# Router logits as float32r products of high and low halves, with the maximum in the adding instruction

## The chip, the core and the metric

The kernel runs on one core of a Trainium2 chip. The time is that of the device, in microseconds (us), from the start of the program to its end; lower is better. Engines: PE (TensorE, matrix products; PEld is its weight load), DVE (VectorE), ACT (ScalarE), POOL (GpSimd) and SP (the queue that issues most DMAs).

## The reference

Three layers one after the other, all in float32: attention with a sliding window and sinks, a mixture of experts with one expert for each token, and a feed-forward layer.

```python
# attention: batch 2, 8 heads, sequence 768, head size 64; keep = 4 sink keys or 128 nearest keys
scores = np.where(keep, scale * np.matmul(q, k.transpose(0, 1, 3, 2)), -1e9)
a = softmax(scores); x = np.matmul(a, v)            # then reshaped to 1536 tokens x 512
# mixture of experts: 8 experts, 512 -> 1024 -> 512
xn = x / (norm(x) + 1e-6); en = expert_emb / (norm(expert_emb) + 1e-6)
logits = xn @ en.T / tau
expert_idx = np.argmax(logits, axis=1)
gate_w = softmax(logits)[chosen]
out[mask] = gate_w[mask, None] * (np.maximum(x[mask] @ w1[e], 0.0) @ w2[e])
# feed-forward: 512 -> 2048 -> 512
h = out @ w_in; y = np.maximum(0.01 * h, h) @ w_out
```

The change is in the router: `logits` for 1536 tokens and 8 experts, and their maximum.

## The kernel before

The program is one stream of instructions per engine. Attention takes the first 140 us or so. It works through 96 items (batch, group of four heads, block of 128 queries, head), and `value` joins four of them to a block. A block of 128 tokens is complete when its second group of heads is done; that makes 12 token tiles, t = 0 to 11. While PE works on scores (L276), transposes of the probabilities (L299) and products with the values (L317, L320) of later items, the router of a finished tile is worked in: three steps later `router_turn`, five steps later `router_logits`.

- `router_turn` (L722) transposes the tile's 512 columns in four pieces into one PSUM tile `xTp` of the pool `ps_t` (4 buffers, shared with all other transposes). ACT copies it to `xT` in SBUF as float32 (L732), then squares the tile for its norm (L739).
- `router_logits` (L742) multiplies the four pieces of `xT`, as stationary operand, with the embeddings `embT` (8 columns) into a PSUM tile `lg` of the pool `ps_sc` (3 buffers, shared with the scores). The profile records each float32 product as two weight loads and two matmuls, so a tile has eight of each. One DVE instruction (L751) copies the logits to SBUF and takes the maximum `top`; L753 to L755 make the index and the one-hot row `oh`, L757 adds it to the count `cum`.
- The last tile (t = 11) is in `HALF`: its first two pieces are transposed and copied eight steps or more earlier, as soon as its first group of heads is done (L337, L338). Only the other half is left for the end.
- After tile 7, `choose` picks the expert that has most tokens so far and has its weights loaded. After tile 9 and after tile 11, `router_rank` (L760, products `rk`) numbers the tokens within their experts. At the end `rank_experts` (L862) counts tokens of each expert from `cum` and `oh` of the last tile (products `cnt`, L874 and L875) and sorts the experts; its result `eid` lets SP load the weights of the next experts.
- The first expert's products (`first_unit`, `ahead`; L1330 writes `hp`) are placed behind the last logits. Some products with no use (`fill`, L841) stand in the gaps.

The order on each engine is fixed before the run. In attention a scheduler settles it from dependencies and its own estimates; an engine then executes strictly in this order. After attention the order on PE is that of the code. The products of attention's scores and most of the experts' and the feed-forward layer's are float32r already, as three products of high and low halves (L1230); ACT writes the high half rounded and DVE the difference.

Of the kernel before, what the change touches and what calls it, by code (L numbers as in the profile page):

```python
# [7 lines left out]
F32 = mybir.dt.float32  # L8
F32R = mybir.dt.float32r
# [6 lines left out]
ALU = mybir.AluOpType  # L16
# [5 lines left out]
P = 128  # L22
# [3 lines left out]
E = 8  # L26
# [4 lines left out]
NTT = NT // P  # L31
# [19 lines left out]
EASE = (4, 5, 6)  # L51
AHEAD = 1
BETWEEN = ("down", 1, 2)
HALF = [NTT - 1]
MAN = set()
STIR = {s: 2 for s in range(9)}
UNITS = [(0, 0, 0, 6), (0, 1, 0, 6), (1, 0, 0, 2), (1, 1, 0, 2), (1, 0, 2, 6), (1, 1, 2, 6)]
# [91 lines left out]
def attention(c, ctx):  # L149
# [109 lines left out]
    def later(n, fn):  # L259

        if n == 0:
            return fn()
        after.append((step[0] + n, c.uid(), fn))
# [47 lines left out]
    def value(b, g, i):  # L311
# [23 lines left out]
        later(1, finish)  # L335
        half = t in HALF
        if g == 0 and half:  # L337
            later(3, lambda: router_turn(c, t, None, (0, 1)))  # L338
        if g == 1:
            if t >= NTT - 2:  # L340
                later(3, lambda: fill(c, c.pst, "t", 1))
            later(3, lambda: router_turn(c, t, None, (2, 3) if half else (0, 1, 2, 3)))
            later(5, lambda: router_logits(c, t))
            if t == T0 - 1:
                later(5, lambda: choose(c))
            if t in RANKS:
                t0 = RANKS[RANKS.index(t) - 1] + 1 if RANKS.index(t) else 0
                if t == NTT - 1:
                    later(7, lambda: rank_experts(c))
                later(7, lambda: router_rank(c, t0, t + 1))  # L350
                if t == T0 - 1:
                    later(7, lambda: choose_rows(c))
            if t == NTT - 1:
                later(3, lambda: first_unit(c))
                later(5, lambda: ahead(c))
# [15 lines left out]
    turn = {(0, 0): group_turns(0, 0)}  # L371
    router_tables(c)
    setting = router_setup(c)
    stir(7)
    n = len(items)
# [242 lines left out]
def router_setup(c):  # L618

    nc, tc = c.nc, c.tc  # L620
    cp = c.const
    rp, emb, tau = c.embs
    sq = rp.tile([E, DM], BF16, name="sq")
    ss = rp.tile([E, 1], F32, name="ss")
    nc.scalar.activation(out=sq, in_=emb, func=AF.Square, accum_out=ss)
    yield
    nrm = norm(c, rp, ss, [E, 1], "e")
    yield
    nc.vector.tensor_scalar(out=nrm, in0=nrm, scalar1=1e-6, scalar2=tau, op0=ALU.add, op1=ALU.mult)
    nc.vector.reciprocal(out=nrm, in_=nrm)  # L630
    nc.vector.tensor_scalar(out=emb, in0=emb, scalar1=nrm, scalar2=None, op0=ALU.mult)
    yield
    t = c.pst.tile([P, 4, E], F32, tag="t", name="embT_ps")
    for kk in range(4):
        nc.tensor.transpose(t[:, kk, :], emb[:, kk * P:(kk + 1) * P], c.ident[0:E, 0:E])
    c.embT = cp.tile([P, 4, E], F32, name="embT")
    nc.vector.tensor_copy(c.embT, t)


def router_tables(c):  # L640
# [65 lines left out]
def norm(c, pool, ss, shape, nm):  # L706

    V = c.nc.vector
    y = pool.tile(shape, F32, name=f"ny_{nm}")
    q = pool.tile(shape, F32, name=f"nq_{nm}")  # L710
    yi = y.bitcast(I32)
    V.tensor_scalar(out=yi, in0=ss.bitcast(I32), scalar1=1, scalar2=None, op0=ALU.logical_shift_right)
    V.tensor_scalar(out=yi, in0=yi, scalar1=float(0x1fbd1df5), scalar2=None, op0=ALU.add)
    for _ in range(3):
        V.reciprocal(out=q, in_=y)
        V.tensor_tensor(out=q, in0=q, in1=ss, op=ALU.mult)
        V.tensor_tensor(out=y, in0=q, in1=y, op=ALU.add)
        V.tensor_scalar(out=y, in0=y, scalar1=0.5, scalar2=None, op0=ALU.mult)
    return y


def router_turn(c, t, pool=None, parts=(0, 1, 2, 3)):  # L722

    nc = c.nc
    pool = pool or c.pst
    x = c.x[t].rearrange("p h d -> p (h d)")
    tp = pool.tile([P, len(parts), P], F32, tag="t", name=f"xTp{c.uid()}")
    for k, kk in enumerate(parts):
        turned = nc.tensor.transpose(tp[:, k, :], x[:, kk * P:(kk + 1) * P], c.ident)  # L729
    if parts[0] == 0:  # L730
        c.xT[t] = c.rt.tile([P, 4, P], F32, tag="xT" if parts[-1] == 3 else "xTh", name=f"xT{c.uid()}", bufs=2 if parts[-1] == 3 else 1)
    first = nc.scalar.copy(out=c.xT[t][:, parts[0]:parts[-1] + 1], in_=tp)  # L732
    if parts[-1] == 3:
        c.x.pop(t)
        c.xT[t] = c.xT[t], turned
        c.turned = turned
        sq = c.rt.tile([P, DM], BF16, tag="sq", name=f"sq{c.uid()}", bufs=1)
        with c.tc.issue_after(first.ins):
            nc.scalar.activation(out=sq, in_=x, func=AF.Square, accum_out=c.ss[:, t:t + 1])  # L739


def router_logits(c, t, pool=None):  # L742

    nc = c.nc
    xT, turned = c.xT.pop(t)
    lp = (pool or c.psc).tile([P, E], F32, tag="sc", name=f"lg{c.uid()}")
    with c.tc.issue_after(turned.ins):
        for kk in range(4):
            c.logged = nc.tensor.matmul(lp, lhsT=xT[:, kk, :], rhs=c.embT[:, kk, :], start=(kk == 0), stop=(kk == 3))  # L749
    lg, top, idx, oh = c.lg[:, t, :], c.top[:, t], c.idx[:, t:t + 1], c.oh[:, t, :]  # L750
    nc.vector.tensor_scalar(out=lg, in0=lp, scalar1=0.0, scalar2=None, op0=ALU.add, op1=ALU.max, accum_out=top)  # L751
    hit = c.rt.tile([P, E], F32, tag="hit", name=f"hit{c.uid()}")
    nc.vector.scalar_tensor_tensor(out=hit, in0=lg, scalar=top, in1=c.em8, op0=ALU.is_equal, op1=ALU.mult)  # L753
    nc.vector.tensor_reduce(out=idx, in_=hit, axis=AX.X, op=ALU.min)
    nc.vector.tensor_scalar(out=oh, in0=c.em8, scalar1=idx, scalar2=None, op0=ALU.is_equal)  # L755
    if t + 1 < NTT:
        nc.vector.tensor_tensor(out=c.cum[:, t + 1, :], in0=c.cum[:, t, :], in1=oh, op=ALU.add)  # L757
# [941 lines left out]
```

## Time and profile before

| | |
|---|---|
| median of 3 runs | 594.13 us (592.95 to 597.09) |
| profiled execution, whole time | 593.38 us |
| its span | 591.6 us |
| PE busy | 579.3 us, 98% of the span |
| PEld busy | 516.1 us, 87% |
| DVE busy | 375.1 us, 63% |
| ACT busy | 278.1 us, 47% |
| POOL busy | 64.7 us, 11% |
| chain that ended last | PE 86%, DVE 4%, issue 3%, DMA 3%, ACT 2% |

The span is the part of the profiled execution that the trace covers; 1.8 us of its time lie outside. Busy shares are means over stages with different limits, so the stretch in question has to be looked at by itself. A busy PE is not a PE at its peak: matmuls are pipelined, and their ends are modelled. The chain shows when each instruction's turn came, so a run of n instructions over a time gives the pace of one.

### The profile page before, as it was taken

How to read it: one execution, taken by the hardware profiler on the slowest of the kernel's cores; microseconds unless marked ns; L12 is line 12 of the kernel's file. 1: busy time of each engine (PE TensorE's matmuls, PEld its weight loads, DVE VectorE, ACT ScalarE, POOL GpSimd, SP SyncE). 2: the span in 40 equal slices, each digit the busy share in tenths (PEclk: the TensorE clock that was granted, in tenths of full speed). 3: DMA queues.
4: the chain of work that ended last, by engine and by line, in shares of the span. 5: the costliest groups of instructions: out<-in, count | busy, mean ns of one | idle time of the engine just before them, and what ended most of it. 6: DMA issues, size and time to landing. Idle time of an engine off the chain costs nothing.

```text
span 591.6 us, 9764 instructions
## 1 busy us (share of the span) xinstructions
PE 579.3 (98%) x3504; PEld 516.1 (87%) x3505; DVE 375.1 (63%) x903; ACT 278.1 (47%) x532; POOL 64.7 (11%) x195
## 2 busy tenths in 40 slices
PE   8999999999999999999999999999999999999995
PEld 5998999999999998899999888888888888888884
DVE  7999699776689966887991799954322223322240
ACT  4878687663476436744552545423322222322220
POOL 6223012121301000010000000000100001100001
PEclk9999999999999999999999999999999999999999
DMA  7646142082295569999977500000100000100001
GB/s 160 154 95 130 61 113 65 24 285 90 77 315 168 157 173 302 350 376 364 377 268 226 202 1 0 2 0 19 54 0 1 0 1 24 48 0 1 0 20 58
DMA packets 75178, 70.44 MB, mean 119 GB/s; under 512 B 41236, under 2 KB 57620, under 8 KB 75120
## 3 DMA queue, kind: packets, MB, share of 16 engines
q1 hardware_dynamic: 72736, 63.07, 34.4%
q0 software_dynamic: 2096, 6.64, 3.4%
q8 instruction: 30, 0.49, 0.3%
q14 instruction: 28, 0.23, 0.1%
q10 hardware_dynamic: 288, 0.00, 0.0%
HBM read 63.41 MB, written 6.29 MB: 118 GB/s over the span
## 4 chain that ended last, share of the span: by engine, by line
PE 86%; DVE 4%; issue 3%; DMA 3%; ACT 2%; SPq 1%; POOL 0%; DVEq 0%; POOLq 0%; ACTq 0%
PE hp L1230 29%; PE acc L1230 28%; PE xp L317 6%; PE hp L1330 4%; PE acc L1348 4%; PE sc L276 4%; PE tp L299 3%; PE lg L749 2%; DMA slot_first<-in_moe_w 1%; PE tq L206 1%; PE xp L320 1%; PE xTp L729 1%; PE tr L1218 1%; PE tk L206 1%; DVE head_k L217 1%
## 5 line engine op out<-in xcount | busy, mean ns | idle before, releaser
L1230 PE MATMUL acc<-slot,h 128*128 128x512 f32 x588 | 142.7, 390 | 0.0
L1230 PE MATMUL hp<-fxT,slot 128*128 128x512 f32 x576 | 137.1, 389 | 0.0
L1230 PEld LDWEIGHTS acc<-slot,h 128*128 128x128 f32 x588 | 109.6, 188 | 22.3
L1230 PEld LDWEIGHTS hp<-fxT,slot 128*128 128x128 f32 x576 | 108.1, 188 | 22.4
L1595 DVE TENSOR_TENSOR lk<-hp,lk 128x512 f32<-128x512 f32 x48 | 32.9, 689 | 97.5 <-ACT lk L1594 97.3
L1594 ACT ACTIVATE lk<-hp 128x512 f32<-128x512 f32 x48 | 28.5, 598 | 110.3 <-PE hp L1230 104.5
L285 ACT ACTIVATE p<-p,los 128x288 f32<-128x288 f32 (+2 forms) x96 | 46.1, 506 | 15.3 <-DVE los L281 14.3
L1150 DVE TENSOR_TENSOR slot<-slot_raw,slot 128x1024 fp32r<-128x1024 f32 x36 | 42.9, 1220 | 4.7 <-ACT slot L1149 4.6
L276 PE MATMUL sc<-head_k,head_q 128*128 128x288 f32 (+1 forms) x192 | 44.9, 332 | 0.6 <-DVE los L281 0.4
L1629 POOL DMA_INDIRECT out_y<-y,sid x12 | 11.7, 978 | 304.2 <-DVE y L1628 282.9
L317 PE MATMUL xp<-v,pt 128*128 128x65 f32 x352 | 44.2, 269 | 0.6 <-DVE x L331 0.5
L317 PEld LDWEIGHTS xp<-v,pt 128*128 128x128 f32 x352 | 42.8, 191 | 1.0 <-PE rk L766 0.6
L1597 DVE TENSOR_TENSOR h<-lk,h 128x512 fp32r<-128x512 f32 x43 | 29.5, 690 | 18.1 <-ACT h L1596 17.9
L1596 ACT CAST h<-lk 128x512 fp32r<-128x512 f32 x43 | 26.7, 622 | 29.2 <-DVE lk L1595 29.2
L1149 ACT CAST slot<-slot_raw 128x1024 fp32r<-128x1024 f32 x36 | 36.0, 1049 | 0.0
L1348 PE MATMUL acc<-h,slot_raw 128*128 128x184 f32 (+2 forms) x192 | 33.8, 320 | 0.1
L276 PEld LDWEIGHTS sc<-head_k,head_q 128*128 128x128 f32 x192 | 29.0, 190 | 3.7 <-DVE los L281 1.3
L1348 PEld LDWEIGHTS acc<-h,slot_raw 128*128 128x128 f32 x192 | 30.7, 190 | 0.4 <-DVE yT L1354 0.4
L1230 PE MATMUL acc<-h,slot 128*128 128x352 f32 (+1 forms) x192 | 30.7, 309 | 0.0
L299 PE MATMUL tp<-ident,p 128*128 128x128 f32 x176 | 29.8, 274 | 0.3 <-ACT pt L302 0.2
L1230 PEld LDWEIGHTS acc<-h,slot 128*128 128x128 f32 x192 | 28.7, 188 | 0.0
L1246 POOL DMA_INDIRECT rows<-xd,ids x15 | 15.5, 1030 | 112.0 <-PE tr L1218 103.3
(294 smaller groups left out, 910.3 us busy)
## 6 DMA issues: line engine op xcount, KB each, us to landing
slot_raw<-in_moe_w SPq DMA_DIRECT2D x48, 512.0 KB
slot_first<-in_moe_w SPq DMA_DIRECT2D x16, 512.0 KB
slot_wide<-in_moe_w_in SPq DMA_DIRECT2D x8, 1024.0 KB
slot_wide<-in_moe_w_out SPq DMA_DIRECT2D x8, 1024.0 KB
raw_k<-in_k SPq DMA_DIRECT2D x32, 96.0 KB
raw_q<-in_q SPq DMA_DIRECT2D x32, 96.0 KB
xd<-x SPq DMA_DIRECT2D x12, 256.0 KB
v<-in_v SPq DMA_DIRECT2D x12, 192.0 KB
```

The lines of the kernel that those rows point to most:

```text
L276: nc.tensor.matmul(sc[:, 0:w], lhsT=qt[:, half, i * P:(i + 1) * P], rhs=kt[:, off:off + w], start=half == 0, stop=half == 1)
L285: c.raised = nc.scalar.activation(out=p, in_=p, func=AF.Exp, scale=-1.0, bias=lo)
L299: nc.tensor.transpose(u.t[:, h % 2, n, :], u.p[:, h, o:o + P], c.ident)
L317: nc.tensor.matmul(xp[:, h, :], lhsT=u.pt[h // 2][:, h % 2, n, :], rhs=vT[b, g][:, kb, h, :], start=h == 0 and n == 0, stop=h == 3 and i < ...
L1149: nc.scalar.copy(out=sl.g[0], in_=raw)
L1150: nc.vector.tensor_tensor(out=sl.g[1], in0=raw, in1=sl.g[0].bitcast(F32), op=ALU.subtract)
L1230: c.nc.tensor.matmul(out, lhsT=a[x], rhs=b[y], start=first and n == 0, stop=last and n == 2)
L1348: nc.tensor.matmul(acc[k], lhsT=g[:, f % 2, k * P:(k + 1) * P], rhs=h, start=f == 0, stop=f == nf - 1)
L1594: nc.scalar.activation(out=raw, in_=hp, func=AF.Copy, scale=0.01)
L1595: nc.vector.tensor_tensor(out=raw, in0=hp, in1=raw, op=ALU.max)
L1596: x = nc.scalar.copy(out=h[:, 0, :], in_=raw)
L1597: y = nc.vector.tensor_tensor(out=h[:, 1, :], in0=raw, in1=h[:, 0, :].bitcast(F32), op=ALU.subtract)
```

## The change

The embeddings are kept twice more: `embR` holds their high half (rounded to float32r) and their low half (the rest) side by side, 16 columns for each of the four pieces. This is done once (two DVE instructions).

For each tile ACT writes the transposed tile's high half instead of a float32 copy, and a new DVE instruction (L737 of the changed kernel) subtracts it from `xTp` to make the low half. The logits come from eight float32r products: four with the high half of x against both halves of the embeddings (128x16), four with the low half of x against the high embeddings (128x8), added in the first 8 of the 16 columns. Then ACT copies the other 8 columns to `lg` (L759), and one DVE instruction with an accumulator (L760) adds both parts and takes the maximum, in place of L751.

`xT` is twice as large and has one buffer instead of two. `HALF` is empty: the last tile is transposed whole after its second group of heads.

```diff
-HALF = [NTT - 1]
+HALF = []
...
     c.embT = cp.tile([P, 4, E], F32, name="embT")
+    c.embR = cp.tile([P, 4, 2, E], F32R, name="embs")
     nc.vector.tensor_copy(c.embT, t)
+    nc.vector.tensor_copy(c.embR[:, :, 0], t)
+    nc.vector.tensor_tensor(out=c.embR[:, :, 1], in0=t, in1=c.embR[:, :, 0].bitcast(F32), op=ALU.subtract)
...
-        c.xT[t] = c.rt.tile([P, 4, P], F32, tag="xT" if parts[-1] == 3 else "xTh", name=f"xT{c.uid()}", bufs=2 if parts[-1] == 3 else 1)
-    first = nc.scalar.copy(out=c.xT[t][:, parts[0]:parts[-1] + 1], in_=tp)
+        c.xT[t] = c.rt.tile([P, 2, 4, P], F32R, tag="xT", name=f"xT{c.uid()}", bufs=1)
+    hi, lo = (c.xT[t][:, h, parts[0]:parts[-1] + 1] for h in range(2))
+    first = nc.scalar.copy(out=hi, in_=tp)
+    nc.vector.tensor_tensor(out=lo, in0=tp, in1=hi.bitcast(F32), op=ALU.subtract)
...
-    lp = (pool or c.psc).tile([P, E], F32, tag="sc", name=f"lg{c.uid()}")
+    lp = (pool or c.psc).tile([P, 2, E], F32, tag="sc", name=f"lg{c.uid()}")
     with c.tc.issue_after(turned.ins):
         for kk in range(4):
-            c.logged = nc.tensor.matmul(lp, lhsT=xT[:, kk, :], rhs=c.embT[:, kk, :], start=(kk == 0), stop=(kk == 3))
+            nc.tensor.matmul(lp.rearrange("p h e -> p (h e)"), lhsT=xT[:, 0, kk, :], rhs=c.embR[:, kk].rearrange("p h e -> p (h e)"),
+                             start=(kk == 0), stop=False)
+        for kk in range(4):
+            c.logged = nc.tensor.matmul(lp[:, 0], lhsT=xT[:, 1, kk, :], rhs=c.embR[:, kk, 0], start=False, stop=(kk == 3))
     lg, top, idx, oh = c.lg[:, t, :], c.top[:, t], c.idx[:, t:t + 1], c.oh[:, t, :]
-    nc.vector.tensor_scalar(out=lg, in0=lp, scalar1=0.0, scalar2=None, op0=ALU.add, op1=ALU.max, accum_out=top)
+    nc.scalar.copy(out=lg, in_=lp[:, 1])
+    nc.vector.tensor_tensor_reduce(out=lg, in0=lp[:, 0], in1=lg, scale=1.0, scalar=-3.0e38, op0=ALU.add, op1=ALU.max, accum_out=top)
```

The scheduler orders attention anew, so lines shift in the whole stage. Three places matter. The first is DVE in the middle of attention, around the end of one tile's index work and the start of the next block's scores (`p` is the masked score tile, `sc` the scores in PSUM). Before:

```order
L755 TENSOR_SCALAR oh<-em_263,idx 128x8
L217 TENSOR_TENSOR head_k_149<-tk_1444,head_k_149 64x384
L217 TENSOR_TENSOR head_k_151<-tk_1444,head_k_151 64x384
L757 TENSOR_TENSOR cum<-cum,oh 128x8
L281 ISA p_1472,los<-sc_1473,ma 128x288
```

And in the changed kernel, at the corresponding place:

```order
L764 TENSOR_SCALAR oh<-em_263,idx 128x8
L737 TENSOR_TENSOR xT_1482<-xTp_1477,xT_1482 128x512
L766 TENSOR_TENSOR cum<-cum,oh 128x8
L281 ISA p_1494,los<-sc_1495,ma 128x288
L281 ISA los 128x1
```

A subtraction of 128x512 now stands in DVE's queue ahead of the masked scores, whose buffers PE waits to get back.

The second place is DVE at the end of attention, around the values of the last tile (`xp_2453` before, `xp_2512` after; `x` is the finished tile, `rec` the reciprocal). Before:

```order
L753 SCALAR_TENSOR_TENSOR hit_2421<-lg,top,em_263 128x8
L754 TENSOR_REDUCE idx<-hit_2421 128x1
L755 TENSOR_SCALAR oh<-em_263,idx 128x8
L757 TENSOR_TENSOR cum<-cum,oh 128x8
L329 TENSOR_SCALAR rec_2458<-xp_2453 128x4
L769 TENSOR_TENSOR sel_2433<-rk_2430,oh 128x16
L330 RECIPROCAL rec_2458<-rec_2458 128x4
L770 TENSOR_REDUCE r<-sel_2433 128x2
L331 TENSOR_TENSOR x_2254<-xp_2453,rec_2458 128x256
```

After:

```order
L762 SCALAR_TENSOR_TENSOR hit_2479<-lg,top,em_263 128x8
L763 TENSOR_REDUCE idx<-hit_2479 128x1
L737 TENSOR_TENSOR xT_2507<-xTp_2502,xT_2507 128x512
L764 TENSOR_SCALAR oh<-em_263,idx 128x8
L329 TENSOR_SCALAR rec_2517<-xp_2512 128x4
L766 TENSOR_TENSOR cum<-cum,oh 128x8
L330 RECIPROCAL rec_2517<-rec_2517 128x4
L778 TENSOR_TENSOR sel_2491<-rk_2488,oh 128x16
L331 TENSOR_TENSOR x_2305<-xp_2512,rec_2517 128x256
```

The subtraction for tile 10 (`xT_2507`) stands ahead of the one-hot row of tile 9, and so ahead of everything that finishes tile 11.

The third place is PE over the same time, from the values of the last tile to its logits. Before:

```order
L729 MATMUL xTp_2444<-ident,x_2207 128x128 x2
L317 MATMUL xp_2453<-v_1608,pt_2384 128x65 x2
L317 MATMUL xp_2453<-v_1608,pt_2402 128x65 x2
L766 LDWEIGHTS tri
L766 MATMUL rk_2430<-oh,tri 128x16
L766 LDWEIGHTS ones
L766 MATMUL rk_2430<-cum,ones 128x16
L749 MATMUL lg_2459<-embT,xT_2449 128x8 x4
L729 MATMUL xTp_2476<-ident,x_2254 128x128 x2
L1218 MATMUL tr_2482<-ident,slot_rows_134 128x128 x4
L749 MATMUL lg_2488<-embT,xT_2284 128x8 x4
```

After:

```order
L317 MATMUL xp_2512<-v_1641,pt_2455 128x65 x2
L775 LDWEIGHTS tri
L775 MATMUL rk_2488<-oh,tri 128x16
L775 LDWEIGHTS ones
L775 MATMUL rk_2488<-cum,ones 128x16
L754 MATMUL lg_2518<-embs,xT_2507 128x16 x4
L757 MATMUL lg_2518<-embs,xT_2507 128x8 x4
L732 MATMUL xTp_2540<-ident,x_2305 128x128 x2
L1227 MATMUL tr_2550<-ident,slot_rows_134 128x128 x4
L754 MATMUL lg_2556<-embs,xT_2545 128x16 x4
L757 MATMUL lg_2556<-embs,xT_2545 128x8 x4
```

The sequence is the same with logits in two groups of four; the first two transposes of the last tile, which stood earlier in attention, now stand just ahead of the logits of tile 9 (`lg_2468`, not shown).

## Rows read from the trace of the kernel before

**Rows 1.** The page's first line: length of the span.

```profile
span 591.6 us, 9764 instructions
```

**Rows 2.** Stretches: length, busy PE, PEld, DVE, ACT, POOL, clock, DMA share, GB/s.

```profile
60.00:70.00 10.00, 10.00 (x87) 9.79 (x86) 5.87 (x24) 5.59 (x14) 1.24 (x6) 1.00 0.19 64
70.00:110.00 40.00, 40.00 (x347) 39.13 (x346) 36.22 (x153) 32.74 (x79) 9.06 (x26) 1.00 0.32 81
...
125.00:140.00 15.00, 15.00 (x128) 14.51 (x128) 8.78 (x42) 9.59 (x26) 0.59 (x2) 1.00 0.72 251
```

**Rows 3.** Chain that ended last, in order: start us, length us, engine and line.

```profile
60.10 0.44 PE xTp L729 x4
60.53 1.73 PE xp L317 x16
...
63.20 0.79 PE lg L749 x8
...
212.29 0.36 PE ipp L1019 x12
...
222.34 1.43 PE hp L1230 x12
```

**Rows 4.** Groups by shape to 240 us: busy us, mean ns | idle before.

```profile
L276 PEld LDWEIGHTS sc<-head_k,head_q 128*128 128x128 f32 x192 | 29.0, 190 | 3.7 <-DVE los L281 1.3 <-DVE head_q L229 0.7 <-issue 0.3
...
L749 PEld LDWEIGHTS lg<-embT,xT 128*128 128x128 f32 x96 | 11.7, 192 | 0.1
...
L1230 PE MATMUL hp<-slot,mxT 128*128 128x256 f32 x48 | 6.6, 287 | 0.0
...
L732 ACT COPY xT<-xTp 128x512 f32<-128x512 f32 x11 | 6.4, 585 | 4.6 <-PE xTp L729 4.5
...
L281 DVE CUSTOM_DVE_ANT_0 p<-sc,m 128x128 f32<-128x128 f32 x16 | 4.5, 283 | 2.2 <-PE sc L276 2.1
L309 ACT COPY ps<-sk 128x128 f32<-128x128 f32 x16 | 4.2, 264 | 3.3 <-PE sk L307 3.2
...
L362 PEld LDWEIGHTS <-warm 128*128 128x128 bf16 x29 | 2.9, 116 | 3.0 <-issue 1.4 <-DVE warm L248 1.2
...
L1223 DVE TENSOR_TENSOR slot_big<-tr,slot_big 128x512 fp32r<-128x512 f32 x3 | 2.0, 679 | 0.0
```

**Rows 5.** The same chain at the end of attention, from tile 9's logits.

```profile
139.10 0.79 PE lg L749 x8
139.90 0.35 PE xTp L729 x2
140.25 0.84 PE xp L317 x8
...
142.02 0.43 PE xTp L729 x2
142.45 0.44 PE tr L1218 x4
142.89 0.79 PE lg L749 x8
...
144.14 1.03 PE hp L1330 x8
145.17 0.01 PE cnt L875
```

**Rows 6.** DVE in order of time there: start us, length us, line, operation.

```profile
141.54 0.42 DVE L331 TENSOR_TENSOR x<-xp,rec 128x256 f32<-128x256 f32 x1
...
143.72 0.17 DVE L751 TENSOR_SCALAR_CACHE_REDUCE lg<-lg 128x8 f32<-128x8 f32 x1 [0.56 <-PE lg L749]
...
144.39 0.23 DVE L755 TENSOR_SCALAR oh<-em,idx 128x8 bf16<-128x8 f32 x1
```

**Rows 7.** ACT in order of time there.

```profile
142.49 0.37 ACT L732 COPY xT<-xTp 128x256 f32<-128x256 f32 x1 [1.00 <-PE xTp L729]
...
143.38 0.58 ACT L1220 COPY slot_x<-tr 128x512 f32<-128x512 f32 x1
```

## The prediction

> **What bounds the kernel now.** I read the stretches first. The router's tiles lie between 60 and 145 us of a span of 591.6 us [rows 1]; whatever this change does, it does there or pushes along from there. In that time PE is the engine without a gap: busy 10.00 of 10.00 us from 60 to 70, 40.00 of 40.00 from 70 to 110, 15.00 of 15.00 from 125 to 140, at a granted clock of 1.00, which is 2.4 GHz [rows 2]. DVE is the engine to look at next. It works 5.87 of 10.00 us from 60 to 70 and 8.78 of 15.00 from 125 to 140, so there it has room; but from 70 to 110 it works 36.22 of 40.00, and only 3.78 us are left [rows 2]. ACT has 7.26 us left in the same 40 us.
>
> Second, the chain in order of time gives PE's pace. Logits of one tile are 8 matmuls in 0.79 us, 0.099 us each, though they have only 8 columns; products with 65 columns are 16 in 1.73 us, 0.108 each; transposes, 128 columns, are 4 in 0.44, 0.110 each [rows 3]. From 8 to 128 columns the pace hardly changes, so the columns don't set it: the load of the 128x128 stationary tile does. A float32r product with 256 columns comes every 1.43/12 = 0.119 us [rows 3, 4]; there the columns begin to count.
>
> Third, the end of attention. It is one chain through PE, DVE and ACT: the last tile's values (140.25), its transposes (142.02), logits (142.89), the one-hot row on DVE (144.39), and then the count product `cnt` at 145.17, from which the experts are ranked [rows 5, 6]. PE goes on with the first expert behind it in a fixed order, so what delays `cnt` delays nearly all that follows.
>
> **The change, part by part.**
>
> *The products.* Eight recorded matmuls in a tile before, eight after: a float32 product is recorded twice (96 for the 48 in the code), a float32r product once (192 for 96 scores of two halves) [rows 4]. What each costs is the question, as no float32r product with few columns is in the trace. Its weight load is: 190 ns on record for the float32r scores against 192 ns for the float32 logits, and 116 ns for 16-bit weights [rows 4]. By that it behaves like the float32 load, so I take 0.099 us for each, and 0 for the part. From above the bound is the 256-column pace: 8 x 0.119 = 0.95 us, +0.16 a tile, +1.9 us for 12. From below it is the 16-bit pace, 12 products in 0.36 us, 0.030 each [rows 3]: 8 x 0.03 = 0.24, -0.55 a tile, -6.6 us for 12.
>
> A rule speaks to this. The Trainium skill (page "TensorE: Matmul & The Clock Gate", section "Weight-path perf modes — Fast Weight Load (FWL) and DoubleRow") has weights of 128 columns loaded fast, about twice as fast as measured there, whenever the input type is not FP32. If float32r does not count as FP32, that would make an estimated 0.05 us a product, 8 x 0.05 = 0.40 in place of 0.79 and -4.7 us for 12 tiles; if it counts, the part is 0. The records of 190 against 192 ns speak for the second [rows 4].
>
> *The subtraction, 12 times.* Its nearest row is the same operation on the same shape in the expert layer: 0.679 us [rows 4]. That is 12 x 0.68 = 8.1 us more for DVE. Two of the twelve fall before 70 us and two between 125 and 140, where the room (4.13 and 6.22 us) is far more than 1.4 us: 0 [rows 2]. If this cover were gone they would cost 0.68 each. Six fall into 70 to 110 us: 4.1 us of work into 3.78 us of room. Nothing can push the cost under 4.1 - 3.78 = 0.3 us; if none of the gaps can be used, it is 4.1. What is late then is the next thing in DVE's queue: as the order shows, the masked scores (which give PE its score buffers back) and the copies that free the transposes' buffers. Both pools serve PE, which has no gap to wait in. The new instruction also holds its own transposes' buffer about 0.7 us longer. I take the middle, +2.0 us, since some gaps are waits for PE at a fixed place in the order and others simply move.
>
> *Small pieces.* The maximum: a two-input instruction with accumulator takes 283 ns at 128 columns [rows 4], the old one 0.17 us at 8 [rows 6]; between these the difference is at most 0.11 us a tile, and shrinks with the columns: 0. The extra copy on ACT lies below the 264 ns of a 128x128 copy [rows 4]; say 0.2 us, 12 x 0.2 = 2.4 us, of which 6 x 0.2 = 1.2 in 70 to 110, in 7.26 us of room [rows 2]: 0. Without that room it would cost 1.2. The two set-up instructions for the embeddings are of the small size, 0.17 us [rows 6]: 0 to 0.3, taken as 0.2. One buffer for `xT` in place of two: in the new order of PE a tile's logits always stand ahead of the next tile's last transposes, so the copy finds it free: 0, and at most an ACT copy of 0.59 us [rows 4] should it wait at the end.
>
> *The end.* I go through the new order with the old durations, from the logits of tile 9 at 139.10 [rows 5].
> 1. Two transposes of tile 11, formerly done earlier, stand ahead: 2 x 0.110 = 0.22. The logits end at 139.10 + 0.22 + 0.79 = 140.11, the transposes of tile 10 at 140.46, the last values (0.84) at 141.30.
> 2. ACT makes the high half of tile 10 by 140.50 + 0.59 = 141.09. DVE's subtraction for it stands ahead of the one-hot row of tile 9: 141.13 to 141.81, the row done by 142.0. PE needs that row for `rk`, so it waits from 141.30 to 142.0. This wait is new.
> 3. Logits of tile 10: 142.04 to 142.83; both halves are there. The last tile's x (0.42 on DVE [rows 6], behind `rec` and `sel`) is ready at about 142.7, so its transposes end at 142.83 + 0.35 = 143.18 (142.45 before) and those of `tr` at 143.62.
> 4. High half of tile 11 on ACT: 143.22 to 143.81 (512 columns, 0.59, where 256 took 0.37 [rows 7]). The four high products fill 143.85 to 144.25, and PE waits for the subtraction, 143.85 to 144.53. The four low ones end at 144.57 + 0.40 = 144.97; before, the logits ended at 143.68.
> 5. The `fill` products and the expert's first eight matmuls (together 145.17 - 143.68 = 1.49 [rows 5]) end at 146.46. `slot_x`, which they read, is on ACT behind the square and done near 145.0: no wait. The maximum comes at 145.2 and the one-hot row 0.90 later [rows 6], at 146.1, in time.
>
> So `cnt` runs at 146.46 in place of 145.17: **+1.3 us**. Under 0.8 (the transposes and the longer copy and subtraction of tile 11 alone) it can't well be; with both last subtractions at full price, 2 x 0.68, the transposes 0.22, the longer ACT copy 0.22 and the new one 0.2 it is 2.0. SP's loads of the next experts wait for `eid`, which comes from `cnt`, and move along with PE, so I credit nothing back.
>
> *Sum.* 0 + 2.0 + 0.2 + 1.3 = +3.5 us. The profiled execution took 593.38 us with a span of 591.6; that makes a span of 595.1 and 596.9 us. It stands 0.75 us below the median of the runs, 594.13, so I forecast **597.6 us**. Its own range, by the bounds of its terms without the two far ones of the products, is 595.2 (0.3 + 0 + 0.8) to 600.5 (4.1 + 0.3 + 2.0).
>
> **Rivals.**
>
> *A, slower: DVE becomes the bound of attention.* The place is DVE's queue from 60 to 145 us, the price all twelve subtractions, 8.1 us, and the end, 1.3 + 0.2: 594.1 + 9.6 = 603.7. For it: six of them exceed the room in their stretch, and PE takes buffers from a pool that DVE frees. Against it: where the other six lie, DVE is busy 59% of the time. It decides, that is, more than 1% is lost, when over 4.4 us of the 8.1 can't be hidden.
>
> *B, hidden.* The gaps of 70 to 110 take the subtractions but for 0.3 us, and only the end is left: 594.1 + 0.3 + 1.3 = 595.7; with the end at its lower bound 595.2. For it: PE, not DVE, has no gap there.
>
> *C, the products do become cheap.* Float32r weights load at the 16-bit pace: -6.6 + 3.5 = -3.1, 591.0; with the rest hidden, -6.6 + 0.3 + 0.8, 588.6. Against it stand the 190 ns of the loads; for it, that no such product with few columns is on record. The Trainium skill's rule named above is this case at half the gain, an estimated 592.9 us.
>
> **How the numbers follow.** Forecast (595.9 to 600.1): 0.43. B (592 to 595.9): 0.22. A (over 600.1): 0.22, and 0.02 for a worse order of the scheduler. C: 0.11, of which 0.05 below 588.2, where the rest would be hidden or the new order is better by itself. A measurement of this kernel can tell about 1%, 5.9 us, from no change: faster, below 588.2, 0.05; within 1%, 0.71; slower, above 600.1, 0.24. The range from 590.5 to 602.5 leaves out about half of C below and half of A above, some 0.18.
>
> **What would show it.** In the profile after: eight matmuls a tile, in 0.75 to 0.95 us (0.4 or less would be C). DVE busier by 8 us in attention, subtractions near 0.68 us, and in the 40 us that held tiles 2 to 7 a busy share near 100%, with PE idle for scores or transposes by some 2 us (5 or more would be A, none B). At the end, PE waiting for DVE ahead of `rk` by some 0.7 us and between the high and low products of tile 11, and `cnt` about 3.5 us later than 145.17. After that all should be moved by that much and not changed. I am wrong if the time after `cnt` changes by more than 1 us, or if PE's stream of logits is not 0.1 us a product.

## The result and the profile after

| | before | changed |
|---|---|---|
| median | 593.63 us (592.95 to 597.24, 17 executions) | 598.31 us (597.73 to 599.95, 17 executions) |
| ratio | | 1.0064, 95% interval 1.0048 to 1.0081 |
| profiled execution, span | 593.38 us, 591.6 us | 598.25 us, 596.5 us |
| mean granted clock of PE in it | 0.998 | 0.993 |

The change costs 0.6% by the ratio and 0.8% (4.7 us) by the medians, within the 1% of "no change", and the time lies 0.7 us above the forecast of 597.6. The sum was nearly right, though its largest term was too large, and one was missing.

One thing has to be known to read all that follows. Executions of the same kernel fall into two groups by their mean granted clock: 0.996 and more, or 0.995 and less. Of the kernel before, 57 of the 84 executions timed beside the changed kernel and the experiments took 592.9 to 594.3 us, and 27 took 595.8 to 597.3. All 17 of the changed kernel are in the lower group by clock. I call the groups *full clock* and *fallen clock*. The mean takes in the end of the program, too: in every profile the clock is at 0.50 for the last 1.7 to 3.6 us, when PE has nothing left to do. So a mean of 0.996 does not rule out a short fall before that.

First the page of the changed kernel: its span and the busy times of the engines.

```profile
span 596.5 us, 9804 instructions
PE 581.5 (97%) x3505; PEld 517.0 (87%) x3505; DVE 382.4 (64%) x917; ACT 279.1 (47%) x543; POOL 64.9 (11%) x195
```

DVE has 7.3 us more than before, PE 2.2 and ACT 1.0. Next the 40 us of [rows 2]: length, busy time of PE, PEld, DVE, ACT and POOL, granted clock, DMA share, GB/s.

```profile
70.00:110.00 40.00, 39.08 (x338) 38.19 (x336) 37.45 (x152) 32.02 (x82) 8.73 (x24) 1.00 0.31 81
```

PE had no gap there and now stands still for 0.92 us; DVE is 1.2 us busier. Third, the groups by shape to 240 us (busy us, mean ns | idle before), which answer to [rows 4].

```profile
L737 DVE TENSOR_TENSOR xT<-xTp,xT 128x512 fp32r<-128x512 f32 x12 | 8.3, 689 | 1.3 <-ACT xT L736 1.1
...
L757 PEld LDWEIGHTS lg<-embs,xT 128*128 128x128 f32 x48 | 6.8, 204 | 0.5 <-DVE xT L737 0.5
L754 PEld LDWEIGHTS lg<-embs,xT 128*128 128x128 f32 x48 | 6.7, 202 | 0.5 <-ACT xT L736 0.5
...
L759 ACT COPY lg<-lg 128x8 f32<-128x8 f32 x12 | 2.0, 166 | 5.6 <-PE lg L757 5.6
L760 DVE CUSTOM_DVE_ANT_0 lg<-lg,lg 128x8 f32<-128x8 f32 x12 | 1.9, 160 | 2.7 <-ACT lg L759 2.7
```

The subtraction takes 0.69 us, the new maximum 160 ns (164 before), the extra copy 166 ns, and a weight load of the new products a little more than the old 192 ns. Fourth, the chain at the end of attention, to be laid beside [rows 5]: start, length, engine and line.

```profile
139.80 0.35 PE lg L754 x4
140.15 0.44 PE lg L757 x4
...
141.54 0.69 DVE xT L737
142.23 0.15 DVE oh L764
...
142.62 0.45 PE lg L754 x4
...
144.48 1.02 PE lg L754 x4
145.50 0.85 PE lg L757 x4
...
147.26 1.92 PE hp L1339 x8
149.17 0.01 PE cnt L884
```

Tile 9's logits take 0.35 + 0.44 = 0.79 us, as before. Those of tile 11 take 1.87, and the first expert's first eight products 1.92 where [rows 5] have 1.03. Nothing waits inside them; PE itself is slower. Stretches of one us show it (same columns):

```profile
141.00:142.00 1.00, 0.72 (x7) 0.60 (x7) 0.85 (x3) 1.00 (x3) 0.00 (x0) 1.00 0.69 262
142.00:143.00 1.00, 0.58 (x7) 0.58 (x6) 1.00 (x7) 0.13 (x2) 0.00 (x0) 1.00 0.00 0
143.00:144.00 1.00, 1.00 (x11) 1.00 (x10) 0.86 (x8) 0.33 (x2) 0.04 (x1) 1.00 0.00 0
144.00:145.00 1.00, 0.76 (x6) 0.53 (x3) 0.93 (x4) 1.00 (x4) 1.00 (x2) 0.56 0.69 262
145.00:146.00 1.00, 1.00 (x7) 1.00 (x6) 0.35 (x2) 0.52 (x2) 0.55 (x1) 0.50 0.00 0
...
150.00:151.00 1.00, 1.00 (x5) 0.64 (x4) 1.00 (x8) 0.00 (x0) 0.00 (x0) 0.52 0.00 0
151.00:152.00 1.00, 1.00 (x11) 1.00 (x11) 0.90 (x6) 0.00 (x0) 0.00 (x0) 1.00 0.00 0
```

PE stands still for 0.28 and 0.42 us between 141 and 143, works a full microsecond, stands still for 0.24, and from 144.1 to 151.0, for 6.8 us, its granted clock is 0.50, that is 1.2 GHz in place of 2.4. In the profiled execution of before the clock stays at 1.00 until 589.0 us, 3.4 us after PE's last product.

**Where the 4.9 us are.** Attention begins at times that differ by a microsecond from one execution to another, so I count from a common point: the start of tile 0's last value products on PE (L320, at 62.10 us before and 61.82 after). From there, by the starts on PE's timeline:

| us from tile 0's last values to | tile 9's logits | `rk` | tile 11's logits | `cnt` | end of the span |
|---|---|---|---|---|---|
| before | 76.84 | 78.83 | 80.63 | 82.91 | 529.5 |
| changed | 77.73 | 80.60 | 82.66 | 87.15 | 534.7 |
| difference | +0.89 | +1.77 | +2.03 | +4.24 | +5.2 |

So the middle costs 0.9 and the waits up to tile 11's logits 2.03 - 0.89 = 1.1. Another 2.2 us are lost between these logits and `cnt`, where PE has no gap and its order of work is as before. Behind `cnt` it is 0.9: 0.6 up to the end of PE's last product, of which the first 2 us run at the lower clock, and 0.3 after it, where PE does nothing (that last part takes 5.9 to 6.5 us in the profiles of all versions). By these differences the lower clock costs 2.8. The profile shows 4.9 rather than 5.2, since this execution came to the common point 0.28 us earlier. The same count for other executions of before (in the experiments) gives 76.82 to 76.84 for tile 9, so it can be read to a few hundredths there.

### The profile page after: what moved, and what is told of

Its sections match the earlier page's. It is cut to its first block, busy times and chain, and to the rows that moved or that the text cites. A ratio compares the mean times of both kernels' runs of the same rounds, so it can differ in the third digit from the quotient of the medians.

```text
span 596.5 us, 9804 instructions
## 1 busy us (share of the span) xinstructions
PE 581.5 (97%) x3505; PEld 517.0 (87%) x3505; DVE 382.4 (64%) x917; ACT 279.1 (47%) x543; POOL 64.9 (11%) x195
## 4 chain that ended last, share of the span: by engine, by line
PE 86%; DVE 7%; ACT 2%; DMA 2%; issue 2%; SPq 0%; POOL 0%; DVEq 0%; POOLq 0%; ACTq 0%
PE hp L1239 28%; PE acc L1239 28%; PE hp L1339 6%; PE acc L1357 5%; PE xp L317 5%; PE sc L276 3%; PE tp L299 3%; DVE head_k L217 1%; DVE p L281 1%; PE xp L320 1%; PE tr L1227 1%; PE tq L206 1%; PE lg L757 1%; DVE head_q L229 1%; PE xTp L732 1%
## 5 line engine op out<-in xcount | busy, mean ns | idle before, releaser
L1239 PE MATMUL acc<-slot,h 128*128 128x512 f32 x588 | 142.7, 391 | 0.0
L276 PE MATMUL sc<-head_k,head_q 128*128 128x288 f32 (+1 forms) x192 | 43.0, 328 | 1.7 <-DVE sel L778 0.7
```

The costliest lines, as they stand in the source:

```text
L276: nc.tensor.matmul(sc[:, 0:w], lhsT=qt[:, half, i * P:(i + 1) * P], rhs=kt[:, off:off + w], start=half == 0, stop=half == 1)
L1239: c.nc.tensor.matmul(out, lhsT=a[x], rhs=b[y], start=first and n == 0, stop=last and n == 2)
```

## Experiments

My theory on seeing this: middle and waits as in the prediction but of other size, and a clock that falls because of the waits. The rivals: the halves of the last tile, no longer done early, cost the time; DVE is the bound; the clock falls for a reason that has nothing to do with the waits. Ratios are to executions of the kernel before that were measured with them on the same chip; their medians were 594.18 (22 executions), 593.45 (29) and 593.41 (16). The versions measured with the 29 (the subtraction twice, the last two tiles without it, the products added to and taken from the kernel before) ran on another chip than the other versions; at full clock the kernel before takes 593.4 us there and 593.3 on the other.

### The last tile's early half alone

The kernel before with one line of the change.

```diff
-HALF = [NTT - 1]
+HALF = []
```

> The kernel before with float32 logits, but the last tile transposed whole at the end. Theory (the new waits for DVE at the end lower TensorE's clock): without the subtractions there is only 0.22 us of transposes moved and an ACT copy longer by 0.22 us, no wait of TensorE over 0.3 us, the clock stays at 1.00 to 150 us; +0.2 to +0.6 us over before. Rival (transposing the last tile late is by itself what costs): +2 us or more, with a clock below 1.00 between 140 and 150 us.

Median 595.61 us of 12, ratio 1.0022 (1.0001 to 1.0044). Six at full clock have a median of 594.3 (before 593.3) and six at fallen clock 596.85 (before 596.5). Its chain at the end, profiled at full clock:

```profile
138.47 0.22 PE xTp L729 x2
138.69 0.79 PE lg L749 x8
...
142.66 1.06 PE lg L749 x8
```

Two transposes now stand ahead of tile 9's logits, yet these come 76.83 us after the common point, as before: what is added there is taken out of the attention ahead. The last logits wait 0.24 us for ACT, and `cnt` is 0.4 later. So this part costs 0.4 in the trace, 1.0 by the medians of executions at full clock. Six fallen clocks in 12 against nine in 22 of before don't show that it makes the clock fall more often. The rival that the last tile's halves carry the loss falls.

### The subtraction in the middle: twice, and not at all

In the changed kernel, the subtraction of tiles 0 to 7 done twice, and left out (these tiles' logits then lack the low half of x, with four products of the high half by the embeddings' low half in its place):

```diff
-    nc.vector.tensor_tensor(out=lo, in0=tp, in1=hi.bitcast(F32), op=ALU.subtract)
+    for _ in range(2 if t < T0 else 1):
+        nc.vector.tensor_tensor(out=lo, in0=tp, in1=hi.bitcast(F32), op=ALU.subtract)
```

```diff
+    if t >= T0:
+        nc.vector.tensor_tensor(out=lo, in0=tp, in1=hi.bitcast(F32), op=ALU.subtract)
...
-            c.logged = nc.tensor.matmul(lp[:, 0], lhsT=xT[:, 1, kk, :], rhs=c.embR[:, kk, 0], start=False, stop=(kk == 3))
+            c.logged = nc.tensor.matmul(lp[:, 0], lhsT=xT[:, int(t >= T0), kk, :], rhs=c.embR[:, kk, int(t < T0)], start=False, stop=(kk == 3))
```

> The changed kernel with the subtraction done twice in tiles 0 to 7, so 0.68 us more of DVE work in each; the second writes the same values. It asks how near DVE is to being the bound from 70 to 110 us. Theory (the middle costs only about 0.5 us, since most of the added work goes into gaps): the second six find less room, the logits of tile 9 come 1 to 3 us later than in the changed kernel (139.8), and the time is 599 to 601 us. Rival (DVE has room enough, the 0.5 us are only the new order): under 0.5 us later.

> The changed kernel without the subtraction in tiles 0 to 7; their second four products take the high half of x and the low half of the embeddings instead, the same count and shape, so the low half of x is left out of these tiles' logits. With the changed kernel (one subtraction, logits of tile 9 at 139.80) and e4_twice (two, 141.41) it makes three points. Theory (DVE's gaps take most of the first, little of the second): the logits of tile 9 come 0.3 to 0.9 us earlier than 139.80. Rival (the middle's cost in the changed kernel is all the subtraction at full price, 4.1 us for the six tiles): 2 us or more earlier. The end is as in the changed kernel, so the clock stays low there, and the time is 597 to 598 us.

Twice: 599.97 us, ratio 1.0103 (1.0071 to 1.0135), four executions. Without: 598.52, ratio 1.0083 (1.0050 to 1.0117), four. All eight have a fallen clock. Tile 9's logits come at 79.07 and 76.90 us from the common point, against 77.73 in the changed kernel and 76.84 before. So the subtractions of the first eight tiles cost 0.83 us, and as many again 1.34. What the stretch from 70 to 110 us shows of this, first without the subtractions, then (two fences) with twice as many:

```profile
70.00:110.00 40.00, 39.83 (x346) 39.23 (x346) 35.72 (x150) 32.70 (x82) 9.04 (x26) 1.00 0.30 80
```

```profile
70.00:110.00 40.00, 38.75 (x326) 37.05 (x325) 37.71 (x150) 30.63 (x77) 8.66 (x24) 1.00 0.30 74
```

PE's idle time goes from 0.17 through 0.92 to 1.25 us, while DVE never gets beyond 37.7 of 40. In the changed kernel five of the subtractions (0.69 each) start in this stretch, yet DVE does only 1.2 us more in it; of the 5.5 us more that it does from 60 to 140, 1.6 lie ahead of the stretch and 2.7 behind it. So other work has moved out of the stretch, to where there is room. DVE is not the bound; rival A falls, with the nearness of the second price to twice the first as a warning.

The scheduler ordered each of these versions anew, so the differences hold what that moved, too. The version without them gains 0.83 us in the middle and yet is no faster than the changed kernel. Its one-us stretches say why:

```profile
141.00:142.00 1.00, 0.43 (x4) 0.31 (x4) 0.92 (x4) 0.83 (x3) 0.00 (x0) 1.00 0.49 186
142.00:143.00 1.00, 0.87 (x9) 0.87 (x8) 0.97 (x8) 0.00 (x0) 0.00 (x0) 0.85 0.00 0
143.00:144.00 1.00, 1.00 (x6) 1.00 (x7) 0.67 (x5) 0.17 (x1) 0.33 (x1) 0.50 0.27 104
```

The wait ahead of `rk` is as long (0.70 us), but the clock falls at 142.7 us, 2.0 us earlier when counted from the common point, and `cnt` is only 0.25 earlier, at 86.90 us from the common point. Its time lies 0.5 us above the range expected for it.

### One wait less: the order on DVE, and the early half again

In the changed kernel, the subtraction of tile 10 put behind the one-hot row of tile 9 (`c.hot`), for which `rk` waits:

```diff
-    nc.vector.tensor_tensor(out=lo, in0=tp, in1=hi.bitcast(F32), op=ALU.subtract)
+    with c.tc.issue_after(c.hot.ins) if t == NTT - 2 else nullcontext():
+        nc.vector.tensor_tensor(out=lo, in0=tp, in1=hi.bitcast(F32), op=ALU.subtract)
```

and, in another version, tile 11's first half again made early, in a tile of its own:

```diff
-HALF = []
+HALF = [NTT - 1]
...
+        c.xTh = c.rt.tile([P, 2, 2, P], F32R, tag="xTh", name="xTh", bufs=1)
```

> The changed kernel with one order on DVE made: the subtraction of tile 10 behind the one-hot row of tile 9. Theory: TensorE's wait ahead of the ranking products falls from 0.7 us to 0.2 to 0.4 us; the wait for the last tile's halves stays. 0.3 us gain by the wait alone, 2 to 3 us if the clock then stays at 1.00. Rival (the middle): no change against the changed kernel.

> The changed kernel with the first half of the last tile transposed, copied and subtracted early again, as before; the rest of the float32r logits is as changed. Theory (clock): the wait ahead of the last logits shrinks by some 0.5 us (256 columns in place of 512 on ACT and DVE); if that keeps the clock at 1.00 the time is +0.8 to +1.5 us over before, if the clock still falls +3 us or more. Rival (the middle of attention, DVE's queue): no gain from this, +3.5 us.

The first: 597.81 us, ratio 1.0069 (1.0046 to 1.0092), five. The second: 597.86, ratio 1.0061 (1.0037 to 1.0084), six. All eleven with a fallen clock. The wait ahead of `rk` is all but gone in both (`rk` at 79.92 and 79.97 us from the common point, 80.60 in the changed kernel); in the second, too, the one-hot row of tile 9 comes ahead of the subtraction of tile 10, by the scheduler's new order. By the medians at most 0.5 us are gained. The stretches of the second show why I can't call the waits the whole cause of the clock:

```profile
141.00:142.00 1.00, 1.00 (x11) 0.99 (x10) 0.59 (x4) 0.41 (x2) 0.00 (x0) 1.00 0.00 0
142.00:143.00 1.00, 1.00 (x12) 0.89 (x10) 0.93 (x4) 0.97 (x3) 0.00 (x0) 1.00 0.69 262
143.00:144.00 1.00, 1.00 (x7) 0.90 (x7) 0.94 (x8) 0.02 (x1) 0.00 (x0) 0.71 0.00 0
```

PE is on record as busy without a gap for two microseconds, and the clock falls nevertheless, at 143.4 us; in the first it falls at 143.1, and there PE has no gap on record either. A wait of some 0.15 us can hide here, since the ends of products are modelled: `rk` starts 0.99 us after the first of the last eight value products, and 0.84 us in the kernel before.

### The waits filled with useless products

In the changed kernel, three products of 512 columns behind the last values and four ahead of the last logits. They change no result.

```diff
+        if g == 1 and t == NTT - 1:
+            with tc.issue_after(c.valued.ins):
+                fill(c, c.pst, "t", 3)
...
+        if t == NTT - 1:
+            fill(c, c.pst, "t", 4)
         for kk in range(4):
```

> The changed kernel with 3 useless products behind the last values and 4 ahead of the last tile's logits, so that TensorE works while it would wait for DVE. Theory (the clock): the waits stay in length but are filled, the clock is 1.00 from 140 to 155 us, the count product comes about 2 us earlier than in the changed kernel and the time is 2 to 3 us lower, +1.0 to +2.0 us over before. Rival (the waits themselves, the clock is no loss because TensorE waits anyway): the same as the changed kernel, +3.8 us, or up to 0.5 us more for the useless products.

Median 595.91 us (595.37 to 596.65), ratio 1.0026 (1.0006 to 1.0046): 2.4 us less than the changed kernel, and all ten executions at full clock (0.997 to 0.999). The chain, then one of the stretches:

```profile
141.22 0.86 PE fill L855 x4
...
143.96 0.86 PE fill L855 x4
144.82 0.34 PE lg L759 x4
145.16 0.44 PE lg L762 x4
145.61 0.47 PE fill L855 x2
146.08 0.89 PE hp L1344 x8
```

```profile
144.00:145.00 1.00, 1.00 (x8) 0.73 (x7) 0.91 (x3) 1.00 (x4) 1.00 (x2) 1.00 0.04 12
```

The last logits take 0.34 + 0.44 again, at a granted clock of 1.00, and `cnt` comes 85.33 us from the common point: 2.42 later than before and 1.82 earlier than in the changed kernel. The end of the span is 2.4 later than before. That is the price, at full clock, of the change and these products together. Behind `cnt` nothing more is lost.

More than the products differs from the changed kernel, though, for the scheduler ordered this version anew. On DVE the one-hot row of tile 9 now comes ahead of the subtraction of tile 10:

```profile
140.70 0.23 DVE L769 TENSOR_SCALAR oh<-em,idx 128x8 bf16<-128x8 f32 x1
...
141.05 0.68 DVE L740 TENSOR_TENSOR xT<-xTp,xT 128x512 fp32r<-128x512 f32 x1
```

So the wait ahead of `rk` would be gone without any products. The four that stand in its place (one of them, and two transposes of tile 11, stood ahead of tile 9's logits in the changed kernel) leave `rk` at 80.64, as late as there; only the wait ahead of the last logits is really filled. The same order on DVE without the products is the first version of the section before, and its clock fell in all five executions, so the order alone does not keep the clock up.

The same with the early half as well (`HALF = [NTT - 1]`, three products at each place) was to gain another 0.3 to 0.6 us:

> The changed kernel with both repairs of the end: the first half of the last tile early again, and useless products, 3 behind the last values and 3 ahead of the last logits. Theory: the clock is at 0.997 or more in all executions, as with the useless products alone, and the shorter wait of the last tile saves 0.3 to 0.6 us against e2_fills (595.9): 595.2 to 595.7 us, still 1.5 to 2.3 us over executions of the kernel before whose clock does not fall (593.3). Rival (the extra work itself, not the end): 598 us.

Median 595.88 us of 12, ratio 1.0030 (1.0012 to 1.0048): nothing gained. `cnt` is at 85.19, 0.14 earlier. Eleven executions have a mean clock of 0.997 or more; the slowest, 596.51 us, has 0.996, so that it may have had a short fall. This version is the early half of the section before plus six products, with the same order of tile 9's row and tile 10's subtraction on DVE: without the products the clock fell in six of six, with them in one of 12 at most. This pair shows best that the products keep the clock up.

### The last two tiles without the subtraction

In the changed kernel, tiles 10 and 11 with the float32 logits of before (one copy on ACT, eight recorded products, the old maximum).

```diff
-    nc.vector.tensor_tensor(out=lo, in0=tp, in1=hi.bitcast(F32), op=ALU.subtract)
+    if t >= NTT - 2:
+        first = nc.scalar.copy(out=c.xT[t][:, 0].bitcast(F32), in_=tp)
+    else:
...
+        for kk in range(4 if t >= NTT - 2 else 0):
+            c.logged = nc.tensor.matmul(lp[:, 0], lhsT=xT[:, 0, kk, :].bitcast(F32), rhs=c.embT[:, kk, :], start=(kk == 0), stop=(kk == 3))
```

> The changed kernel with float32 logits, one copy and no subtraction for tiles 10 and 11 alone; the last tile is still transposed whole. Theory (nearly all is lost at the end): the waits of TensorE there go back to those of the kernel before with an empty HALF, the mean granted clock is at 0.997 to 0.999 in about half of the executions, and these take 594 to 595.5 us; the others 597 to 598. Rival (the middle): the clock low in all, 598 us.

Median 596.25 us of 12 (594.73 to 598.06), ratio 1.0030 (1.0010 to 1.0050). Mean clocks go from 0.993 to 0.998, without the gap between the two groups. Four executions, not half, have 0.997 or more (594.7 to 595.7 us); the rival, a low clock in all of them, is not borne out either. In its profile (mean clock 0.996) tile 9 is where the changed kernel has it (77.71) and `rk` 0.67 earlier; the clock falls later, at 145.9 us, and for 3.4 us in place of 6.8. Of the 2.1 us between the two versions 0.7 is there at `rk`; the rest goes with the later and shorter fall.

### The same on the kernel before

If useless products keep the clock up, they should do so in the kernel before, where it falls in a third of the executions; and taking out its four (L841) should let it fall more often. First: two more behind the last values, and one ahead of the last logits. Second: without the two single ones near the end and the pair in `ahead`.

```diff
+            with tc.issue_after(c.valued.ins):
+                fill(c, c.pst, "t", 2)
...
+        if t == NTT - 1:
+            fill(c, c.pst, "t", 1)
```

```diff
-            if t >= NTT - 2:
-                later(3, lambda: fill(c, c.pst, "t", 1))
...
-        fill(c, c.pst, "t", 2)
```

> The kernel before with 3 useless products behind the last values (one of them was there, earlier) and 1 ahead of the last logits. Theory (before, too, loses its clock at the end in those executions whose mean granted clock is 0.993, 9 of 22, at 596.5 us against 593.25): with TensorE kept at work all executions have 0.997 or more and take 593.3 to 594.0 us, no more at 596.5. Rival (that clock falls somewhere else): the same two groups, each 0.3 to 0.7 us later.

> The kernel before without the four useless products that it has at the end of attention, ahead of the first expert. Theory (clock): TensorE waits in their place, nothing else is earlier, the clock falls in more executions than before or in all, and the median is 596 us or more. Rival: up to 0.9 us less, as four products of 0.22 us are gone.

More: 594.22 us of 12 (593.23 to 595.02), ratio 1.0002 (0.9986 to 1.0018), all 12 at full clock. By the ratio nothing is gained or lost, and the median lies 0.8 us above that of the kernel before (593.45); but the executions near 597 are gone: the products cost some 0.6 us (`cnt` at 83.54 against 82.91) and save 3 in one execution of three. In the kernel before PE is busy 1.00 of each us from 139 to 145, so these products fill no wait that the profile shows: they are added work. Fewer: 594.70 of 12 (592.73 to 596.73), ratio 1.0013 (0.9994 to 1.0032), six at full clock (median 593.56) and six at fallen clock (595.68). I had expected a median of 596 or more; half against a third is too little to tell with 12 executions. So adding goes with a clock that stays up (12 of 12, against 22 of 29 beside it) at no gain in time, and taking away is not shown to harm.

Last, two plain executions of the kernel before, to see one of each group.

> The kernel before once more, for its profile. Theory: if its mean granted clock is 0.993, the profile shows the clock at half for several us around 140 to 150 us, and the time is 596.5 us; if it is 0.997, the clock is 1.00 there, 593.3 us. Rival: the clock falls elsewhere in the program.

> The same as b1_before, a second profile: by its mean granted clock either 596.5 us with the clock at half around 140 to 150 us, or 593.3 us without.

They took 593.96 us (0.7 more than expected) and 596.25 us, with mean clocks of 0.999 and 0.993. The second one's stretches and chain:

```profile
140.00:141.00 1.00, 1.00 (x13) 1.00 (x12) 0.79 (x5) 0.90 (x2) 0.00 (x0) 1.00 0.56 215
141.00:142.00 1.00, 1.00 (x9) 0.91 (x9) 0.99 (x9) 0.30 (x2) 0.00 (x0) 0.87 0.13 47
142.00:143.00 1.00, 1.00 (x6) 1.00 (x7) 0.90 (x8) 0.45 (x2) 0.52 (x1) 0.50 0.37 141
```

```profile
140.94 0.89 PE lg L749 x8
...
143.37 1.51 PE lg L749 x8
...
145.75 1.91 PE hp L1330 x8
147.66 0.01 PE cnt L875
```

To 141 us both do the same things at the same distances (tile 9's logits 76.82 us from the common point in both), and PE has no gap. Then one keeps its clock and the other loses it for 6.8 us, from 141.7 us on: `cnt` at 85.52 against 82.89, the end of the span 2.5 us later.

## Why the prediction was right, and where it was not

**The products: right.** Eight in 0.79 us, as taken. That pace and the loads of 202 and 204 ns, where 16-bit weights have 116 [rows 4], settle rival C. The Trainium skill's rule that non-FP32 weights load fast (page "TensorE: Matmul & The Clock Gate", section "Weight-path perf modes — Fast Weight Load (FWL) and DoubleRow") gives nothing here: by these loads float32r goes with FP32. (The prediction calls the rule's case half the gain of C; by its own figures, 4.7 against 6.6 us, it is seven tenths.) At the lower clock the stream was not 0.1 us a product, one of my marks: tile 11's eight took 1.87 us.

**The subtractions: too dear.** I took 2.0 us, and the trace has 0.89 at tile 9, of which the version without subtractions puts 0.83 down to them. The 0.2 for the set-up can't be seen: its two instructions run at 49.6 and 51.5 us, ahead of the common point, which comes no later than before. The row I used, 3.78 us of room against 4.1 of work, treats the stretch as closed. It isn't: five of the six subtractions started in it, the sixth at 112.6 us, and other work of DVE moved on to where there is time. PE's idle time was to be some 2 us and is 0.92; DVE's share of the stretch was to be near 100% and is 94%.

**The waits at the end: right in sum.** 1.3 worked out up to `cnt`, 1.1 measured up to tile 11's logits. The wait ahead of `rk`, which I put at 0.7 us, reads on PE's timeline (in brackets: idle before, and its releaser; the last line is DVE's subtraction for tile 11):

```profile
142.42 0.17 PE L775 MATMUL rk<-oh,tri 128*128 128x16 bf16 x1 [0.70 <-DVE oh L764]
...
144.48 1.02 PE L754 MATMUL lg<-embs,xT 128*128 128x16 f32 x4 [0.24 <-ACT xT L736]
...
144.60 0.69 DVE L737 TENSOR_TENSOR xT<-xTp,xT 128x512 fp32r<-128x512 f32 x1
```

Two details were wrong. The 0.22 us for the two moved transposes counts nothing, since they are saved earlier; the first experiment shows it. And the low products of tile 11 don't wait for the subtraction, since the high ones take 1.02 us at the lower clock; the wait is ahead of the high ones. At the full clock, by an estimate, there would have been such a wait: four high products (0.35 us, as in tile 9) would end near 144.85, and the subtraction ends at 145.29, 0.4 later. By that the waits up to `cnt` are worth 1.5 us, and the lower clock 2.4 in place of 2.8.

**The clock: not in the sum.** The step that failed is the one that goes "through the new order with the old durations". I had read the clock of 1.00 in [rows 2] as a given. They end at 140 us; behind that the clock falls in some executions of the kernel before and in all of the changed one. The new order brings PE's clock to 1.2 GHz for 6.8 us, and that costs 2.4 to 2.8 us. That the clock is the cause of these is shown by the version with useless products (same subtractions and copies, all ten at full clock, 2.4 us faster), by the early half without and with products (597.86 and 595.88 us), and by the two plain executions of the kernel before, where the same stream of instructions took 2.5 us longer from the common point with a fall of the same length.

| us | forecast | measured |
|---|---|---|
| middle | 2.0 | 0.9 |
| set-up | 0.2 | not seen |
| waits at the end | 1.3 | 1.1 to 1.5 |
| clock | 0 | 2.8 to 2.4 |
| behind PE's last product | 0 | 0.3 |
| sum | 3.5 | 5.2 (4.9 in the profiled times) |

An excess of 1.3 in the first terms hid part of the term that was missing: that the time came within 0.7 us of the forecast is luck. My marks could hardly tell this: `cnt` was to be 3.5 us later and is 4.0 by the times of the two traces, and behind it 0.9 changes where I had set the limit at 1. Only the marks for the stretch in the middle (PE's idle time and DVE's share), the wait between the high and the low products, and the pace of tile 11's products were plainly missed.

**The base.** I took the median of three executions as one state of the kernel; by their times (592.95, 594.13, 597.09) they held both. Like with like, at full clock before takes 593.3 us (13 executions) and the changed work with the useless products 595.9, +2.7; of the executions measured beside the changed kernel, the six of before near 597 have a median of 597.0, and the changed kernel's 598.3 is +1.3. The rest of the measured difference is that the clock now falls every time, and not in a third of the executions.

**What stays open.** What makes the clock fall in one execution of the kernel before and not in the next. The Trainium skill (page "TensorE: Matmul & The Clock Gate", section "HAM oscillation — how this bites in real kernels") puts such falls down to PE idling between bursts. The fall at the very end of every profile, 2.4 to 4.7 us after PE's last product, agrees with that. At the end of attention the longest idle time before a fall is 0.70 us, and there are falls with none on record (the order on DVE and the early half; the second plain execution), so idle time alone doesn't explain it. The rival that the clock falls for a reason other than the waits therefore stands. What the runs do show is that it falls in the stretch of narrow products and waits at the end of attention, in all 36 executions of the changed kernel and of its variants with neither filled waits nor float32 logits for the last tiles, less surely in the kernel before, and in none of 34 with more 512-column products, one of these (0.996) not being certain. Whether the waits or the narrowness of the products make the difference isn't shown: in the kernel before the added products kept the clock up where no wait was on record. Other work in their place wasn't tried.

## What to carry to other kernels

Where one engine carries a stretch without gaps, price a new wait not only by its length but by what it may do to that engine's clock: here an order with 1.1 to 1.5 us of new waits came with some 2.5 us of slower products, though the runs don't show that the waits are what lowered the clock. Look at the granted clock in stretches of one microsecond, and at the spread of executions by mean clock, before a median is taken as the base of a sum; a few useless products can be worth more than they cost (2.4 us less in the changed kernel, nothing in the kernel before). And room on a busy engine is not closed at the edges of the stretch in which one has read it: ask which result the next engine really waits for.

## What the hardware showed that was not expected

- The same instruction stream, at the same times to 0.02 us up to tile 10's logits, ended attention with PE's clock at 2.4 GHz in one execution and at 1.2 GHz for 6.8 us in another (`cnt` at 82.89 and 85.52 us from the common point).
- A gain ahead of such a fall can be lost in it: leaving out eight subtractions brought tile 9 forward by 0.83 us, the clock fell 2.0 us earlier, and the time was 598.5 against 598.3 us.
- Float32r products with 16 and 8 columns keep the pace of the float32 ones, four in 0.35 and 0.44 us, with weight loads of 202 and 204 ns on record.
